# Attention and two feed-forward layers on one core: state products and attention steps moved within a block

## The chip, the core and the metric

One Trainium2 chip, one of its cores. The metric is the device time of one execution in microseconds (us). The kernel's time before is 1480.17 us, the median of three runs (1479.89 to 1481.52).

## The reference

An attention of tokens against 32 state vectors per head, and back, followed by two feed-forward layers over all 8 x 544 = 4352 rows, all in float32:

```python
# x: B=8, H=8, S=512, D=64; state: B, H, Ns=32, D
scores = scale * x @ state.T;    a  = softmax(scores)   # over the 32 states
xread  = a @ state
scores2 = scale * state @ x.T;   a2 = softmax(scores2)  # over the 512 tokens
sread  = a2 @ x
y = concat([xread, sread], axis=2)      # (B, H, 544, 64) -> (4352, 512)
y = (silu(y @ w_gate) * (y @ w_val)) @ w_out            # 512 -> 1536 -> 512
h = y @ w_in
y = (max(h, 0) + alpha * min(h, 0)) @ w_out2            # 512 -> 2048 -> 512
```

## The kernel before

Each large product is made of three passes over float32 values split in two parts (hi and lo, fp32r), so every operand is copied to a hi part by ScalarE (ACT) and its rest is subtracted by VectorE (DVE) or GpSimd (POOL). The first feed-forward layer runs in nine blocks: blocks 0 to 7 are the eight batches with 512 token rows each, the last one holds the 256 rows of sread. The second layer follows and is not touched.

In a block the first layer's input is never formed. Since xread is a @ state, the block multiplies state with the weights first (the **state products**: state_times_w, L381 on TensorE, into two aux buffers of PSUM; then ScalarE's copies and VectorE's subtractions make sw) and then sw with a. Two hidden columns of 128 form a column pair j, and sw of pair j serves steps 2j and 2j+1.

A block has twelve steps f (Block from L397, ffn1 from L445). A step is, on TensorE: gate (6 matmuls into g, L410), value (6 into v, L410), and project (12 matmuls into acc0 to acc3, L434) of the step before. On the other engines: ScalarE's SiLU of g (s, L417), VectorE's product with v (L420), ScalarE's hi part of the hidden column (h, L76), VectorE's lo part (h, L82). Step 0 finishes the block before instead: its last project, then four copies of its accumulators (xo, two by VectorE, L79, two by ScalarE, L76) and their stores. The next block's first project starts new sums in the same four accumulators.

All else is put into slots (f, 0) behind the gate, (f, 1) behind value and split, and (f, 2) behind project. ffn1_slots (from L509) fills them for a block b: state_times_w of pairs 1 to 5 and, at (10, 2), of pair 0 of the next block; the **attention of the next batch** in two head groups u and v, each in five stages: x transposed (xt, L147), scores (L152) with their maxima and exponentials, the scalings with the transposes of the second softmax (L201, aux, then e2t by VectorE), sread (L211), and the split of a (at, a). Blocks 2 to 6 also convert the second layer's weights (raw L246 and L247 on ScalarE, m L252 and L254 on VectorE, L262 on POOL) and split them (sc L329, sp).

TensorE's order is the program's order (manual_schedule). ScalarE, VectorE, POOL and SP get an order from the tile framework's scheduler, which is fixed when the kernel is built; each engine runs its own row in order. aux has two buffers used in turn by state products, scores, transposes and sread; g, v and each accumulator have one.

Of the kernel before, what the change touches and what calls it, by code (L numbers as in the profile page):

```python
# [25 lines left out]
def attention_and_two_ffns(ctx: ExitStack, tc: tile.TileContext, x, state, w_gate, w_val,  # L26
# [76 lines left out]
    def load_state(b, eng=nc.sync):  # L103
        t = sm.tile([P, H, Ns], F32, tag="st", name=name("st"), bufs=1)
        for hp in range(2):
            for e in range(2):
                q = 64 * hp + 32 * e
                eng.dma_start(t[q:q + 32], state[b, :, :, 32 * e:32 * e + 32].rearrange("h n d -> n h d"))
        for hp in range(2):
            q = slice(64 * hp, 64 * hp + 64)  # L110
            for jj in range(2):
                h = 4 * jj + 2 * hp
                nc.vector.transpose(out=bd[b % 2][q, jj, :, Ns * hp:Ns * hp + Ns], in_=t[q, h:h + 2])
        stt[b] = sm.tile([P, H, Ns], F32, tag="stt", name=name("stt"), bufs=2)
        nc.vector.transpose(out=stt[b].rearrange("p h n -> p (h n)"), in_=t.rearrange("p h n -> p (h n)"))

    def load_xq(b, g, jj):
        t = t2([P, S // 32, 32], F32, "xq")
        for hp in range(2):
            for e in range(2):  # L120
                q = 64 * hp + 32 * e
                nc.sync.dma_start(
                    t[q:q + 32],
                    x[b, 4 * jj + 2 * hp + g].rearrange("(t i) d -> i t d", i=32)[:, :, 32 * e:32 * e + 32])
        xq[b, g, jj] = t

    def load_xn(b, g):
        t = t4([P, SC, 4, D], F32, "xn")
        for h in range(4):
            nc.sync.dma_start(t[:, :, h], x[b, 2 * h + g].rearrange("(p c) d -> p c d", c=SC))  # L130
        xn[b, g] = t
# [257 lines left out]
    def state_times_w(b, j):  # L389
        us = [StateTimesW(b, j, g) for g in range(NG)]  # L390
        for u in us:
            u.product()
        for u in us:
            u.parts()
# [70 lines left out]
    with tc.manual_schedule(engines={mybir.EngineType.PE}):  # L465
# [43 lines left out]
        def ffn1_slots(b):  # L509
            slots = {}  # L510

            def put(f, i, th):
                slots.setdefault((f, i), []).append(th)

            if b == 0:
                for f in range(NF1):
                    for i in range(3):
                        put(f, i, stream1.step)
                    if f % 2 == 1:
                        put(f, 1, lambda f=f: stream1.until(3 * (f // 2) + 2, 2))  # L520
                for g in range(NG):
                    put(0, 0, att[0, g].second_scale)
                    put(0, 1, att[0, g].second_read)
            for j in range(1, NJ1):
                if b == 0:
                    put(2 * j - 1, 2, lambda j=j: stream1.until(3 * j + 1, 1))
                    put(2 * j - 1, 2, lambda j=j: state_times_w(0, j))
                else:
                    put(2 * j - 1, 1, lambda j=j: state_times_w(b, j))
            if b == 1:  # L530
                put(8, 0, lambda: stream2.load(1))
            if 1 < b < B - 1:
                for f in range(NF1):
                    if f % 3 != 0:
                        put(f, 1, stream2.step)
                    put(f, 2, one_later)
            if b == B - 1:
                for f in range(NF1):
                    put(f, 2, one_later)
                gen = load_xs()  # L540
                for f in range(4, 8):
                    put(f, 0, lambda: next(gen))
                put(NF1 - 3, 1, lambda: split_w(0))
                put(NF1 - 2, 1, lambda: split_w(1))
            if b + 1 < B:
                nb = b + 1
                put(0, 0, lambda: load_state(nb))
                u, v = att[nb, 0], att[nb, 1]
                for g in range(NG):
                    def load(g=g):  # L550
                        if nb >= XT:
                            for jj in range(2):
                                load_xq(nb, g, jj)
                        load_xn(nb, g)

                    put(*((2 * g, 2 * g) if b == 0 else (6 * g, 0)), load)
                stages = [[lambda: u.xt(0), lambda: u.xt(1)],
                          [u.scores, u.first_cols, u.second_max, u.first_max, u.second_exp, u.first_exp],
                          [u.first_scale, u.second_scale], [u.second_read], [u.first_parts],
                          [lambda: v.xt(0), lambda: v.xt(1)],  # L560
                          [v.scores, v.first_cols, v.second_max, v.first_max, v.second_exp, v.first_exp],
                          [v.first_scale, v.second_scale], [v.second_read], [v.first_parts]]
                if b == 0:
                    places = [(f, 0) for f in range(5)] + [(6, 1), (7, 0), (8, 1), (9, 0), (9, 2)]
                else:
                    places = [(f, 0) for f in (1, 2, 3, 4, 5, 7, 8, 9, 10, 11)]
                for place, stage in zip(places, stages):
                    for th in stage:
                        put(*place, th)
                put(NF1 - 2, 2, lambda: state_times_w(nb, 0))  # L570
            return slots
# [12 lines left out]
        def load_xs():  # L584
            if not xs:
                xs.append(t8([P, NPAIR, 2, NS], F32R, "xs"))
            for r in range(NS // P):
                t = t2([P, DM], F32, "xsn")
                nc.sync.dma_start(t, srd[r * P:(r + 1) * P, :])
                yield  # L590
                pt = aux([P, NPAIR, P])
                for c in range(NPAIR):
                    nc.tensor.transpose(pt[:, c, :], t[:, c * P:(c + 1) * P], ident)
                acopy(xs[0][:, :, 0, r * P:(r + 1) * P], pt)
                sub_lo(xs[0][:, :, 1, r * P:(r + 1) * P], pt, xs[0][:, :, 0, r * P:(r + 1) * P])
                yield

        def split_w(f):
            t = t8([P, NPAIR, 2, 2, P], F32R, "ws")
            src = wraw[f // 2][:, :, :, (f % 2) * P:(f % 2) * P + P]  # L600
            acopy(t[:, :, 0], src)
            sub_lo(t[:, :, 1], src, t[:, :, 0])
            ws[f] = t

        blocks = [block(b) for b in range(B)]
        for b in range(B):
            ffn1(blocks[b], ffn1_slots(b), (lambda: blocks[b - 1].finish(b - 1)) if b else None)
# [203 lines left out]
        for t, (pr, s) in enumerate(STEPS):  # L811
# [5 lines left out]
            todo, places = list(work), [0]  # L817
# [46 lines left out]
```

## Time and profile before

| | us |
|---|---|
| median of three runs | 1480.17 |
| the profiled execution, its own time | 1480.67 |
| its span | 1478.8 |
| TensorE busy (share of the span) | 1420.6 (96%) |
| VectorE busy | 960.4 (65%) |
| ScalarE busy | 525.0 (35%) |
| POOL busy | 209.6 (14%) |

The span is from the first to the last instruction. A timeline row gives start, length, engine, line, output and input, and in brackets the idle time just before it with what ended it. Matmul lengths are modelled and overlap, so the distance between the starts of two rows says more than a length. An engine's share over the whole span mixes stages: the table says which engine to look at, and the timeline where it waits.

### The profile page before, as it was taken

The numbers are of one execution on the slowest core, as the hardware profiler recorded it, in microseconds if no ns is written. First come the engines' busy times: TensorE is split into PE (matmuls) and PEld (weight loads), VectorE is DVE, ScalarE is ACT, GpSimd is POOL, SyncE is SP. The second block draws the span as 40 slices with busy tenths as digits, with TensorE's granted clock in tenths as the row PEclk, the third lists the DMA queues.
The fourth block names the chain that finished last, engine by engine and source line by source line (L and its number), as shares of the span: only waits on it lengthen the run. The fifth ranks groups of instructions, "written<-read, shape, count | busy, mean of one in ns | idle before, by whom it ended". The sixth has DMA issues, their size and how long they took to land.

```text
span 1478.8 us, 18980 instructions
## 1 busy us (share of the span) xinstructions
PE 1420.6 (96%) x7352; PEld 1105.9 (75%) x7352; DVE 960.4 (65%) x1583; ACT 525.0 (35%) x826; POOL 209.6 (14%) x173
## 2 busy tenths in 40 slices
PE   4888999999999999999999999999999999999997
PEld 1556777667677666777997888888888888888886
DVE  6797545676667777533656678666885669666663
ACT  4874445455455544433522112211221113211111
POOL 4686001222233323100000000000000000000000
PEclk6898999999999999999999999999999999999999
DMA  8351223365544544310255433653256434634455
GB/s 273 110 200 34 58 52 105 101 182 172 146 156 150 165 141 139 87 44 1 86 213 217 160 107 116 226 214 132 99 199 232 156 107 164 218 135 152 138 208 210
DMA packets 160595, 214.65 MB, mean 145 GB/s; under 512 B 103160, under 2 KB 104184, under 8 KB 155384
## 3 DMA queue, kind: packets, MB, share of 16 engines
q1 hardware_dynamic: 159416, 213.30, 42.9%
q8 instruction: 58, 0.95, 0.3%
q14 instruction: 33, 0.27, 0.1%
q10 hardware_dynamic: 1088, 0.13, 0.1%
HBM read 169.88 MB, written 43.52 MB: 144 GB/s over the span
## 4 chain that ended last, share of the span: by engine, by line
PE 86%; DVE 9%; issue 1%; ACT 1%; DMA 1%; SPq 0%; DVEq 0%; ACTq 0%
PE acc L434 17%; PE acc L739 13%; PE aux L739 12%; PE g L410 9%; PE v L687 9%; PE v L410 8%; PE aux L687 6%; PE g L687 6%; PE aux L381 3%; DVE m L252 2%; DVE m L254 2%; PE aux L152 1%; DVE sc L329 1%; PE v L789 1%; PE g L789 1%
## 5 line engine op out<-in xcount | busy, mean ns | idle before, releaser
L434 PE MATMUL acc<-h,wp 128*128 128x512 f32 (+1 forms) x1296 | 306.4, 386 | 8.4 <-ACT xo L76 8.4
L434 PEld LDWEIGHTS acc<-h,wp 128*128 128x128 f32 x1296 | 234.9, 191 | 83.0 <-issue 21.0
L76 ACT ACTIVATE h<-m 128x512 fp32r<-128x512 f32 (+1 forms) x144 | 87.6, 609 | 448.3 <-DVE m L672 443.6
L739 PE MATMUL acc<-wo,h 128*128 128x512 f32 x864 | 219.9, 390 | 2.0 <-ACT h L76 1.7
L739 PE MATMUL aux<-wo,h 128*128 128x512 f32 x768 | 194.9, 389 | 0.0
L739 PEld LDWEIGHTS acc<-wo,h 128*128 128x128 f32 x864 | 161.1, 188 | 35.5 <-ACT h L76 2.1
L693 DVE TENSOR_TENSOR u<-v,p 128x512 f32<-128x512 f32 x96 | 66.3, 690 | 168.4 <-PE v L687 167.8
L739 PEld LDWEIGHTS aux<-wo,h 128*128 128x128 f32 x768 | 144.1, 188 | 30.0
L410 PE MATMUL g<-a,sw 128*128 128x512 f32 x576 | 154.5, 403 | 9.2 <-ACT sw L76 6.7
L410 PE MATMUL v<-a,sw 128*128 128x512 f32 x576 | 156.5, 408 | 0.0
L420 DVE TENSOR_TENSOR s<-s,v 128x512 f32<-128x512 f32 (+1 forms) x108 | 70.0, 648 | 121.4 <-PE v L410 111.6
L687 PE MATMUL v<-x,w 128*128 128x512 f32 x576 | 146.2, 389 | 0.0
L410 PEld LDWEIGHTS g<-a,sw 128*128 128x128 f32 x576 | 109.3, 193 | 47.0 <-ACT sw L76 13.0
L410 PEld LDWEIGHTS v<-a,sw 128*128 128x128 f32 x576 | 108.3, 194 | 33.9 <-issue 10.5
L687 PEld LDWEIGHTS v<-x,w 128*128 128x128 f32 x576 | 108.1, 188 | 22.5
L417 ACT ACTIVATE s<-g 128x512 f32<-128x512 f32 (+1 forms) x108 | 62.0, 574 | 146.7 <-PE g L410 140.6
L82 DVE TENSOR_TENSOR h<-m,h 128x512 fp32r<-128x512 f32 (+1 forms) x144 | 94.7, 658 | 16.1 <-ACT h L76 12.8
L76 ACT ACTIVATE h<-s 128x512 fp32r<-128x512 f32 (+1 forms) x108 | 65.4, 606 | 103.1 <-DVE s L420 103.1
L82 DVE TENSOR_TENSOR sw<-aux,sw 128x512 fp32r<-128x512 f32 x96 | 63.2, 681 | 53.2 <-ACT sw L76 53.1
L687 PE MATMUL g<-x,w 128*128 128x512 f32 x384 | 97.6, 389 | 0.0
L687 PE MATMUL aux<-x,w 128*128 128x512 f32 x384 | 97.4, 389 | 0.0
L82 DVE TENSOR_TENSOR h<-s,h 128x512 fp32r<-128x512 f32 (+1 forms) x96 | 66.7, 695 | 35.8 <-ACT h L76 33.3
(105 smaller groups left out, 1656.8 us busy)
## 6 DMA issues: line engine op xcount, KB each, us to landing
w<-w2d SPq DMA_DIRECT2D x64, 896.0 KB, 6.4
wo<-wo2d SPq DMA_DIRECT2D x40, 1024.0 KB, 6.8
w2d<-sp SPq DMA_DIRECT2D x32, 512.0 KB, 2.9
raw<-in_moe_w_out_dram SPq DMA_DIRECT2D x14, 1024.0 KB, 7.8
out_dram<-o SPq DMA_DIRECT2D x34, 256.0 KB, 2.3
xn<-in_x_dram SPq DMA_DIRECT2D x64, 128.0 KB, 3.0
x2d<-xo SPq DMA_DIRECT2D x32, 256.0 KB, 2.5
raw<-in_moe_w_in_dram SPq DMA_DIRECT2D x8, 1024.0 KB, 9.8
```

Source lines behind the costliest of these rows:

```text
L76: return nc.scalar.activation(o, i, AF.Copy)
L82: (eng or nc.vector).tensor_tensor(out=o, in0=src, in1=hi.bitcast(F32), op=ALU.subtract)
L252: nc.vector.tensor_scalar(out=m, in0=hi, scalar1=0x0FFFFFFF, scalar2=3, op0=ALU.bitwise_and, op1=ALU.logical_shift_left)
L254: nc.vector.scalar_tensor_tensor(out=m, in0=hi, scalar=-0x80000000, in1=m, op0=ALU.bitwise_and, op1=ALU.bitwise_or)
L381: nc.tensor.matmul(self.o[Ns * c:Ns * (c + 1), :], stt[b][q, 2 * c + g, :], wraw[j][q, c].rearrange("p k f -> p (k f)"), start=True, stop= ...
L410: nc.tensor.matmul(o[:, :self.n], self.lhs(f, k, a, which), self.rhs(k, c), start=(i == 0), stop=(i == last))
L417: nc.scalar.activation(self.p[f], self.product(f, 0, "g"), AF.Silu)
L420: nc.vector.tensor_tensor(out=self.p[f], in0=self.p[f], in1=self.product(f, 1, "v"), op=ALU.mult)
L434: nc.tensor.matmul(self.acc[e][:, :self.n], wo1[f // 2][:, f % 2, a, e * P:(e + 1) * P], t[:, c, :self.n], start=(f == 0 and i == 0), stop ...
L687: nc.tensor.matmul(o, w[a][:, q, c], x[k][:, q, e], start=start and n == 0, stop=stop and n == 5, skip_group_check=True)
L693: nc.vector.tensor_tensor(out=o, in0=x0, in1=x1, op=ALU.add)
L739: nc.tensor.matmul(o, h[:, c, a, u * P:(u + 1) * P], wos2[t][:, f, q], start=start and f == 0 and i == 0, stop=stop and f == 1 and i == 2)
```

## The change

Two places in ffn1_slots, and nothing else. For blocks 1 to 7 the state products of pair j stand in slot (2j-2, 2), behind the project of the even step before, instead of (2j-1, 1); for j = 1 that is behind the copies of the finished block's sums in the program. For blocks 1 to 6 the attention's ten stages go from steps 1, 2, 3, 4, 5 and 7, 8, 9, 10, 11 to 2, 3, 5, 6, 6 and 6, 7, 9, 10, 10, and the second head group's loads of x go from step 6 to step 4. Block 0 keeps its order.

```diff
                 else:
-                    put(2 * j - 1, 1, lambda j=j: state_times_w(b, j))
+                    put(2 * j - 2, 2, lambda j=j: state_times_w(b, j))
...
-                    put(*((2 * g, 2 * g) if b == 0 else (6 * g, 0)), load)
+                    put(*((2 * g, 2 * g) if b == 0 else (4 * g, 0)), load)
...
                 else:
-                    places = [(f, 0) for f in (1, 2, 3, 4, 5, 7, 8, 9, 10, 11)]
+                    places = [(f, 0) for f in (2, 3, 5, 6, 6, 6, 7, 9, 10, 10)]
```

TensorE in block 4, steps 0 and 1, before, from the gate of step 0 to the first project of the block (acc with the numbers 478 to 481 are the sums of block 3, 617 begins those of block 4):

```order
L410 MATMUL g_3339<-a_519_2909,sw_3273 128x512 x6
L410 MATMUL v_3373<-a_519_2909,sw_3273 128x512 x6
L434 MATMUL acc_478_2683<-h_3309,wp_1111 128x512 x3
L434 MATMUL acc_479_2684<-h_3309,wp_1111 128x512 x3
L434 MATMUL acc_480_2685<-h_3309,wp_1111 128x512 x3
L434 MATMUL acc_481_2686<-h_3309,wp_1111 128x512 x3
L410 MATMUL g_3413<-a_519_2909,sw_3273 128x512 x6
L410 MATMUL v_3425<-a_519_2909,sw_3273 128x512 x6
L381 MATMUL aux_3437<-wr_296,stt_2580 32x512 x4
L381 MATMUL aux_3442<-wr_296,stt_2580 32x512 x4
L434 MATMUL acc_617_3459<-h_3381,wp_298 128x512 x3
```

The same stretch with the change:

```order
L410 MATMUL g_3339<-a_532_2985,sw_3277 128x512 x6
L410 MATMUL v_3373<-a_532_2985,sw_3277 128x512 x6
L434 MATMUL acc_476_2679<-h_3309,wp_1111 128x512 x3
L434 MATMUL acc_477_2680<-h_3309,wp_1111 128x512 x3
L434 MATMUL acc_478_2681<-h_3309,wp_1111 128x512 x3
L434 MATMUL acc_479_2682<-h_3309,wp_1111 128x512 x3
L381 MATMUL aux_3409<-wr_296,stt_2580 32x512 x4
L381 MATMUL aux_3414<-wr_296,stt_2580 32x512 x4
L410 MATMUL g_3428<-a_532_2985,sw_3277 128x512 x6
L410 MATMUL v_3436<-a_532_2985,sw_3277 128x512 x6
L434 MATMUL acc_615_3455<-h_3381,wp_298 128x512 x3
```

The two products L381 moved from behind step 1's gate and value to ahead of them. ScalarE's row of this stretch has the two sw copies, then the two xo copies, then step 1's SiLU, before and with the change.

ScalarE in block 4, from the SiLU of step 2 (g_3480) to the parts sp of step 3, before:

```order
L417 ACTIVATE s_3479<-g_3480 128x512
L194 ACT_TABLE_LOAD
L194 ACTIVATE e_628_3499,r_629_3500<-aux_3488,m_626_3493 128x512
L167 ACTIVATE s_625_3491<-s_625_3491 128x512
L76 ACTIVATE h_3511<-s_3479 128x512
L417 ACT_TABLE_LOAD
L417 ACTIVATE s_3535<-g_3536 128x512
L76 ACTIVATE sw_3569<-aux_3570 128x512
L76 ACTIVATE h_3566<-s_3535 128x512
L76 ACTIVATE sw_3569<-aux_3575 128x512
L76 ACTIVATE sp_3596<-sc_3530 128x512
```

The same stretch with the change, from the SiLU of step 2 (g_3476); e and r belong to the scores of step 3:

```order
L417 ACTIVATE s_3475<-g_3476 128x512
L76 ACTIVATE h_3496<-s_3475 128x512
L417 ACTIVATE s_3535<-g_3536 128x512
L76 ACTIVATE sw_3515<-aux_3516 128x512
L76 ACTIVATE sw_3515<-aux_3521 128x512
L194 ACT_TABLE_LOAD
L194 ACTIVATE e_637_3555,r_638_3556<-aux_3544,m_635_3549 128x512
L167 ACTIVATE s_634_3547<-s_634_3547 128x512
L76 ACTIVATE h_3567<-s_3535 128x512
L76 ACTIVATE sp_3582<-sc_3530 128x512
```

The exponentials moved from step 2 to step 3, and the sw copies of pair 2 stand behind the SiLU of step 3, ahead of the exponentials. Blocks 3 and 5 have this row too; in blocks 1, 2 and 6 the two sw copies stand ahead of step 3's SiLU. VectorE's row with the change has, in blocks 3 to 6, six operations on the second layer's weights (L252, L329, L254, L329, L329, L329) between the hidden part of step 2 and the subtractions of these sw copies.

ScalarE in block 4 with the change, from the SiLU of step 4 (g_3593) to that of step 5 (g_3668):

```order
L417 ACTIVATE s_3592<-g_3593 128x512
L246 ACTIVATE raw_3447<-raw_3447 128x1024
L76 ACTIVATE h_3624<-s_3592 128x512
L247 ACTIVATE raw_3447<-raw_3447 128x1024
L76 ACTIVATE sw_3647<-aux_3648 128x512
L246 ACTIVATE raw_3627<-raw_3627 128x1024
L76 ACTIVATE sw_3647<-aux_3653 128x512
L247 ACTIVATE raw_3627<-raw_3627 128x1024
L417 ACTIVATE s_3667<-g_3668 128x512
```

The same stretch before, from the SiLU of step 4 (g_3607) to that of step 5 (g_3675):

```order
L417 ACTIVATE s_3606<-g_3607 128x512
L246 ACTIVATE raw_3649<-raw_3649 128x1024
L247 ACTIVATE raw_3649<-raw_3649 128x1024
L76 ACTIVATE h_3646<-s_3606 128x512
L417 ACTIVATE s_3674<-g_3675 128x512
```

The first sw copy of pair 3 moved to behind one pair of raw conversions and ahead of step 5's SiLU; its second copy stands between the next two conversions. Before, these copies came behind step 5's SiLU.

## Rows read from the trace of the kernel before

**Rows 1.** The page, part 1: busy us (share of the span) xinstructions.

```profile
PE 1420.6 (96%) x7352; PEld 1105.9 (75%) x7352; DVE 960.4 (65%) x1583; ACT 525.0 (35%) x826; POOL 209.6 (14%) x173
```

**Rows 2.** Timeline of PE: the first gates of blocks 1, 2, 4, 5 and 7.

```profile
146.54 1.52 PE L410 MATMUL g<-a,sw 128*128 128x512 f32 x6
...
224.46 1.52 PE L410 MATMUL g<-a,sw 128*128 128x512 f32 x6
...
387.46 1.52 PE L410 MATMUL g<-a,sw 128*128 128x512 f32 x6
...
472.47 1.52 PE L410 MATMUL g<-a,sw 128*128 128x512 f32 x6
...
641.25 1.52 PE L410 MATMUL g<-a,sw 128*128 128x512 f32 x6
```

**Rows 3.** Timeline of PE: first projects of blocks 3, 4, 6; at 390.18 block 3's last.

```profile
315.20 3.00 PE L434 MATMUL acc<-h,wp 128*128 128x512 f32 x12 [2.11 <-ACT xo L76]
...
390.18 2.88 PE L434 MATMUL acc<-h,wp 128*128 128x512 f32 x12
...
398.91 4.57 PE L434 MATMUL acc<-h,wp 128*128 128x512 f32 x12 [2.11 <-ACT xo L76]
...
568.99 4.34 PE L434 MATMUL acc<-h,wp 128*128 128x512 f32 x12 [2.10 <-ACT xo L76]
```

**Rows 4.** Timeline of ACT, block 4, step 1: copies of sums.

```profile
396.84 1.08 ACT L76 ACTIVATE sw<-aux 128x512 fp32r<-128x512 f32 x2 [4.47 <-PE aux L381]
397.81 1.09 ACT L76 ACTIVATE xo<-acc 128x512 f32<-128x512 f32 x2
```

**Rows 5.** Windows behind the waits: stretch, busy us per engine (x instructions), PEclk, DMA, GB/s.

```profile
315.00:320.00 5.00, 4.80 (x22) 3.51 (x22) 4.67 (x9) 2.24 (x5) 0.00 (x0) 1.00 0.90 313
...
400.00:405.00 5.00, 5.00 (x17) 3.66 (x18) 3.37 (x6) 1.28 (x3) 0.00 (x0) 0.70 1.05 340
```

**Rows 6.** Timeline of PE: products in block 1; scores and products in block 4.

```profile
207.64 1.09 PE L381 MATMUL aux<-wr,stt 64*32 64x512 f32 x16
...
404.77 1.08 PE L152 MATMUL aux<-xt,bd 128*64 128x512 f32 x4
...
445.03 1.85 PE L152 MATMUL aux<-xt,bd 128*64 128x512 f32 x4
...
455.68 1.06 PE L381 MATMUL aux<-wr,stt 64*32 64x512 f32 x8 [0.28 <-DVE e2t L79]
```

**Rows 7.** Timelines of PE, ACT and DVE, block 4, from the products of step 10.

```profile
465.87 1.09 PE L381 MATMUL aux<-wr,stt 64*32 64x512 f32 x16
466.88 1.65 PE L410 MATMUL g<-a,sw 128*128 128x512 f32 x6
...
467.06 1.09 ACT L76 ACTIVATE sw<-aux 128x512 fp32r<-128x512 f32 x2 [2.02 <-PE aux L381]
468.63 0.60 ACT L417 ACTIVATE s<-g 128x512 f32<-128x512 f32 x1 [0.49 <-PE g L410]
...
467.69 1.29 DVE L82 TENSOR_TENSOR sw<-aux,sw 128x512 fp32r<-128x512 f32 x2 [1.93 <-ACT sw L76]
```

**Rows 8.** Timeline of DVE, block 4: first and last of six operations in a row.

```profile
408.98 0.93 DVE L252 TENSOR_SCALAR m<-raw 128x512 int32<-128x512 int32 x1
...
411.03 1.40 DVE L329 TENSOR_TENSOR sc<-m,sc 128x128 f32<-128x128 f32 x1
```

**Rows 9.** Timeline of ACT, block 4, steps 2 and 3, around the exponentials.

```profile
408.54 1.28 ACT L194 ACT_TABLE_LOAD   x1 [3.07 <-DVE m L189]
409.83 0.69 ACT L194 ACTIVATE e<-aux,m 128x512 f32<-128x512 f32 x1
...
412.97 0.60 ACT L417 ACTIVATE s<-g 128x512 f32<-128x512 f32 x1
...
416.30 0.62 ACT L76 ACTIVATE sp<-sc 128x512 fp32r<-128x512 f32 x1
...
417.44 1.15 ACT L246 ACTIVATE raw<-raw 128x1024 f32<-128x1024 f32 x1
```

## The prediction

> **What bounds the kernel now.** The page comes first. TensorE is busy for 96% of the span [rows 1], so a change of order can only win TensorE's waits, its slow clock, and what a late second operand adds inside a group.
>
> The PE timeline gives these block by block. Each of the blocks 1 to 6 issues the same TensorE work, and its length is the distance between the first gates of two blocks. Block 1 takes 224.46 - 146.54 = 77.92 us and has no wait in it. Block 4 takes 472.47 - 387.46 = 85.01 us. The five blocks 2 to 6 together take 641.25 - 224.46 = 416.79 us, and five times 77.92 is 389.60: **27.2 us are lost in them** [rows 2]. That is all this change can win.
>
> Where it goes: in step 1 of block 4 the first projection of the block starts 2.11 us late, released by ScalarE's copies xo, and its 12 matmuls then take 4.57 us where others take 2.88. Block 3 has the same wait without the slow part [rows 3]; block 6 looks like block 4 (2.10 and 4.34 us), and block 5 repeats block 4. ScalarE shows why. It stood idle for 4.47 us until the state products L381 were done, copied their two sums (sw), and only then copied xo [rows 4]. The block's sums were complete when the last projection ended, before step 1's gate; the copies that free them stand behind copies whose data comes two products later. The slow part is the clock: 0.70 of full speed in the 5 us after the wait of block 4, thus mostly the 1.2 GHz level, against 1.00 after that of block 3 [rows 5].
>
> The rest is lost around the attention's steps. The 16 matmuls of L381 run through in 1.09 us in block 1; in step 9 of block 4 their second half waits until VectorE has copied e2t out of the other aux buffer. Block 4's scores take 1.08 us in step 2 and 1.85 in step 8, where their second half waits [rows 6].
>
> **The change, part by part.** No instruction is added or removed. The state products of pair j go from the middle of step 2j-1 to the end of step 2j-2; the attention's steps go to 2, 3, 5, 6, 6, 6, 7, 9, 10, 10; the second head group's loads go from step 6 to step 4.
>
> *The copy wait goes.* With the products directly behind the last projection, gate and value of step 1 lie between them and the next projection. From an existing place with products ahead of a gate: products at 465.87, gate at 466.88, ScalarE's copies at 467.06 (1.19 us after the products), VectorE's subtractions at 467.69 [rows 7]. With 0.5 us between ScalarE's copies, xo is copied 2.1 to 3.2 us after the products start; VectorE's two copies follow its two subtractions (1.8 and 2.4 us after the products), the first ending at some 3.65 us. The projection wants it at 1.0 + 1.5 + 1.4 = 3.9 us. That is covered by 0.2 us; the next three accumulators have 0.7 us more each. Gain: four waits, 8.4 us, and the slow clock behind three of them, 1.69 + 1.69 + 1.46 = 4.8 us, together 13.2.
>
> *The attention's waits go.* No L381 follows transposes within a step any more, and transposes come two steps after their scores. That is the other 27.2 - 13.2 = 14.0 us. Part of it comes back, as follows.
>
> *A new wait at step 3.* Products fill both aux buffers at the end of step 2, and the scores of step 3 want the older one after a single gate. In blocks 3 to 5 ScalarE's row has step 3's SiLU ahead of the sw copies. By rows 7 the SiLU starts 468.63 - 465.87 = 2.76 us after the products, the first copy 0.5 us later, the subtraction that frees the buffer 0.63 us after that and 0.69 us long: free at 4.6 us. TensorE is there at 466.88 + 1.49 - 465.87 = 2.5 us. So the **scores wait 2.1 us in each of three blocks, 6.3 us**. This follows from the order and the rows, so I give it no lower end. In block 6 the copies stand ahead of the SiLU, but VectorE's subtractions stand behind six operations on the second layer's weights, which took 411.03 + 1.40 - 408.98 = 3.45 us in block 4 [rows 8]; without the stretched ones about 1.9 us. That ends 2 to 3.6 us after the products, the buffer is free at 2.6 to 4.3: between 0 and 1.8 us of wait; I take 1.2, nearer to the measured row. In blocks 1 and 2 neither stands in the way: nothing.
>
> *Steps 5, 7 and 9.* The same pair of buffers meets the transposes of 5 and 9 and the scores of 7. At step 5 ScalarE has, from the exponentials of step 3 on, two table loads, two exponentials, a hidden half and a SiLU (412.97 + 0.5 - 408.54 = 4.9 us [rows 9]), three parts of split weights (417.44 - 416.30 = 1.1), another hidden half (0.5) and two raw conversions (1.15 each, about 1.05 from start to start), 8.6 us. It starts 408.54 - 404.77 = 3.8 us after the scores, or 3.2 where no weight operation of VectorE's comes between, so it reaches the copy at 11.8 to 12.4. TensorE issues the products 1.0 + 1.5 + 2.7 + 1.4 + 1.4 + 2.8 = 10.8 us after the scores (scores, value, projection, gate, value, projection), and their sums are there 1.1 us later, at 11.9. So 0 to 0.5 us late; steps 7 and 9 come to 0 to 0.6. Nine places in blocks 3 to 5: 0 to 5.4 us; I take 0.2 each, 1.8.
>
> A rule speaks against this term. Here a table load takes 1.28 us and the exponential behind it starts 0.01 us after its end [rows 9]. The Trainium skill, page "ScalarE: Activation LUTs", section "What ACT_TABLE_LOAD costs", puts a drain of about 1380 ns beside the 1283 ns of every switch. The trace agrees with the load and shows no drain; with it the copies of steps 5 and 9 would come some 2.8 us later. I keep the row.
>
> *The clock.* Of the four waits of 2.1 us, three were followed by the slow level. Of the three new ones I take two, at 1.69 us: 3.4 us; the ends are none, and all four (with block 6), 6.8 us.
>
> *Queues.* The second group's loads are wanted two steps after their issue instead of one, each step being some 7 us (85.01 / 12). SP's queue holds them behind the same stores of split weights as before. That costs nothing; if the stores were late, x's transposes of step 6 and then the scores of step 7 would be. POOL's subtract and scale keep their neighbours and have a step more.
>
> **Sum.** 27.2 - 6.3 - 1.2 - 1.8 - 3.4 = **14.5 us won**. The profiled execution took 1480.67 us (span 1478.8): 1466.2. It lies 0.5 us above the median: **1465.7 us**. Its own ends: 27.2 - 6.3 = 20.9 won, 1459.3; and 27.2 - 6.3 - 1.8 - 5.4 - 6.8 = 6.9 won, 1473.3.
>
> **Rivals.**
> 1. *The scores do not wait.* If the buffer they take were free already, the 1.2 and 1.8 us of the other terms stay at most: 27.2 - 3 = 24 won, **1456**. Against it: the products take both buffers just before.
> 2. *The copy wait stays.* The change promises to free the accumulators in time, yet ScalarE and VectorE still have sw ahead of xo in every block but the last. If those copies come as late as before, the 13.2 us stay lost and 1.3 us are won: **1479**. For it: a cover of only 0.2 us. Against it: the products are 2.8 us earlier, and a miss of that cover costs tenths.
> 3. *ScalarE loses steps 5, 7 and 9: slower.* If there, too, the SiLU or the raw conversions run first, nine places lose 2.1 us and half of them the clock, 2.1 + 0.8 = 2.9 each, 26 us against 14.5 + 1.8: **1490**. It decides from (14.5 + 1.8) / 9 = 1.8 us a place. For it: at step 5 ScalarE arrives within half a microsecond of being late. Against it: its rows have the copies ahead of the SiLU there.
> 4. *A table switch costs twice its load.* Two more loads of 1.28 us ahead of the copies of steps 5 and 9, six places in blocks 3 to 5: 15.4 us, **1481**. Against it: the 0.01 us of rows 9. This is what the Trainium skill's drain ("ScalarE: Activation LUTs") would amount to.
>
> **How the numbers follow.** A measurement of this kernel tells 0.2%, 3 us, from no change. Forecast 0.74; rival 1 0.08, rival 2 0.07, rival 3 0.07, rival 4 0.04. Forecast and rival 1 are faster: 0.82; rivals 2 and 4 make no difference: 0.11; rival 3 is slower: 0.07. The forecast's ends with rival 1 hold 0.82, so the range goes from 1456 to 1474.
>
> **What would show it.** In step 1 of blocks 3 to 6 the first projection has no idle time from xo and takes 2.9 us. In step 3 of blocks 3 to 5 the scores wait some 2.1 us for VectorE's sw, in block 6 less, in blocks 1 and 2 not. No L381 waits for e2t. Blocks 1 and 2 take 77.9 us, blocks 3 to 5 some 81 to 83, block 6 about 79. It is wrong if the scores of step 3 don't wait, if xo still ends a wait of TensorE, or if steps 5, 7 or 9 lose more than a microsecond.

## The result and the profile after

The changed kernel takes **1467.6 us**, the median of four runs (1466.17 to 1469.5), against 1480.03 of the kernel before in the same set of runs (1479.11 to 1481.52): the ratio is 0.9916, with a 95% interval of 0.9899 to 0.9933. That is 12.4 us won; 14.5 were forecast, and the time lies inside the range of 1456 to 1474.

The profiled execution took 1469.5 us, with a span of 1467.3. The page, part 1, of the changed kernel, to be set beside [rows 1]:

```profile
PE 1408.8 (96%) x7352; PEld 1100.2 (75%) x7352; DVE 963.7 (66%) x1583; ACT 524.3 (36%) x826; POOL 210.8 (14%) x173
```

TensorE has the same 7352 matmuls and is busy 11.8 us less, though its share of the span is the same 96%: what the slow clock and late operands added inside groups counted as busy time, too. Windows from the first gate of block 2 to that of block 7, before and after (stretch, busy us of PE, PEld, DVE, ACT and POOL, PEclk, DMA, GB/s):

```profile
224.46:641.25 416.79, 406.06 (x2321) 288.76 (x2320) 278.42 (x506) 209.88 (x344) 108.43 (x94) 0.99 0.44 136
...
225.72:629.77 404.05, 393.59 (x2321) 283.00 (x2320) 279.52 (x506) 208.34 (x344) 109.70 (x94) 1.00 0.46 141
```

TensorE's idle time in these five blocks is 416.79 - 406.06 = 10.7 us before and 404.05 - 393.59 = 10.5 after. The change took the old waits away and made new ones of nearly the same sum; what was won is busy time that the slow clock and stretched groups (as the scores of step 8, 1.85 us where others take 1.08 [rows 6]) had cost. The share hides this; the distances between blocks show the gain. The timeline of PE with the first gates of blocks 1, 2, 4, 5 and 7, as in [rows 2]:

```profile
147.60 1.52 PE L410 MATMUL g<-a,sw 128*128 128x512 f32 x6
...
225.72 1.52 PE L410 MATMUL g<-a,sw 128*128 128x512 f32 x6
...
385.56 1.52 PE L410 MATMUL g<-a,sw 128*128 128x512 f32 x6
...
468.87 1.52 PE L410 MATMUL g<-a,sw 128*128 128x512 f32 x6
...
629.77 1.52 PE L410 MATMUL g<-a,sw 128*128 128x512 f32 x6
```

Blocks 2 to 6 take 629.77 - 225.72 = 404.05 us, where they took 416.79: 12.7 won. Block 4 takes 83.31, where it took 85.01. Blocks 1 and 2, which have no wait now, take 78.12 and 78.10, so the new order costs 0.2 us a block by itself. Block 1 starts 1.06 us later than before; block 0 was not changed, and in a second profile of the same kernel (experiment 8) block 1 starts at 146.93, so this is the spread of the beginning.

What is left of the loss, 404.05 - 5 x 77.92 = 14.4 us, is four kinds of waits. The timeline of PE, steps 3, 7 and 9 of block 3, then step 3 of blocks 4 to 6:

```profile
326.12 1.08 PE L152 MATMUL aux<-xt,bd 128*64 128x512 f32 x4 [1.90 <-DVE sw L82]
...
354.10 1.08 PE L152 MATMUL aux<-xt,bd 128*64 128x512 f32 x4 [0.82 <-DVE sw L82]
...
367.94 0.72 PE L201 MATMUL aux<-ident,e 128*128 128x128 f32 x4 [0.41 <-DVE sw L82]
...
407.84 1.93 PE L152 MATMUL aux<-xt,bd 128*64 128x512 f32 x4 [1.90 <-DVE sw L82]
409.70 2.40 PE L410 MATMUL v<-a,sw 128*128 128x512 f32 x6
...
491.14 1.08 PE L152 MATMUL aux<-xt,bd 128*64 128x512 f32 x4 [1.90 <-DVE sw L82]
...
571.97 1.08 PE L152 MATMUL aux<-xt,bd 128*64 128x512 f32 x4 [0.97 <-DVE sw L82]
```

The scores of step 3 wait 1.90 us in blocks 3 to 5 and 0.97 in block 6, always for VectorE's sw. In block 4 alone the scores themselves then take 1.93 us where others take 1.08, and value 2.40: the slow clock. Steps 7 and 9 of blocks 4 and 5 look like those of block 3 (0.83 and 0.90 us, 0.41 and 0.42). No first project of a block waits, and no L381 waits for e2t.

### The profile page after: what moved, and what is told of

Its sections match the earlier page's. It is cut to its first block, busy times and chain, and to the rows that moved or that the text cites. A ratio compares the mean times of both kernels' runs of the same rounds, so it can differ in the third digit from the quotient of the medians.

```text
span 1467.3 us, 19014 instructions
## 1 busy us (share of the span) xinstructions
PE 1408.8 (96%) x7352; PEld 1100.2 (75%) x7352; DVE 963.7 (66%) x1583; ACT 524.3 (36%) x826; POOL 210.8 (14%) x173
## 4 chain that ended last, share of the span: by engine, by line
PE 83%; DVE 10%; ACT 4%; issue 2%; DMA 1%; SPq 0%; DVEq 0%; ACTq 0%
PE acc L434 14%; PE acc L739 13%; PE aux L739 12%; PE v L687 9%; PE v L410 9%; PE g L410 8%; PE aux L687 6%; PE g L687 6%; PE aux L381 2%; DVE m L252 2%; DVE m L254 2%; PE aux L152 1%; DVE sw L82 1%; PE v L789 1%; PE g L789 1%
## 5 line engine op out<-in xcount | busy, mean ns | idle before, releaser
L434 PE MATMUL acc<-h,wp 128*128 128x512 f32 (+1 forms) x1296 | 298.2, 379 | 0.0
L410 PE MATMUL g<-a,sw 128*128 128x512 f32 x576 | 158.1, 408 | 9.7 <-ACT sw L76 6.4
L410 PEld LDWEIGHTS g<-a,sw 128*128 128x128 f32 x576 | 105.6, 191 | 74.2 <-issue 28.5
L82 DVE TENSOR_TENSOR h<-s,h 128x512 fp32r<-128x512 f32 (+1 forms) x96 | 63.3, 659 | 40.6 <-ACT h L76 38.3
```

Source lines behind the costliest of these rows:

```text
L82: (eng or nc.vector).tensor_tensor(out=o, in0=src, in1=hi.bitcast(F32), op=ALU.subtract)
L410: nc.tensor.matmul(o[:, :self.n], self.lhs(f, k, a, which), self.rhs(k, c), start=(i == 0), stop=(i == last))
L434: nc.tensor.matmul(self.acc[e][:, :self.n], wo1[f // 2][:, f % 2, a, e * P:(e + 1) * P], t[:, c, :self.n], start=(f == 0 and i == 0), stop ...
```

## The experiments

The theory to be tested has three parts. ScalarE, VectorE and TensorE each run their own row in order, so a wait is set by what stands ahead of the sw copies in a row, and not only by when the products come. The move of the products frees the accumulators. The attention's new places are what keeps the aux buffers from meeting once the products have moved. The earlier loads of x belong to the second edit and were not tested apart from it. The rivals: that one of the two edits is the whole gain; that the products still come too late for the scores; that ScalarE's own backlog from the exponentials makes the late waits. Where nothing else is said, an experiment differs from the changed kernel by the lines shown. Experiments 1 to 4, 5 to 8 and 9 were run in three further sets, in which the kernel before took 1479.9, 1480.97 and 1481.12 us, where it took 1480.03 beside the changed kernel: a difference between runs of two sets can be off by about 1 us.

**1. The products alone** (difference to the kernel before):

```diff
-                    put(2 * j - 1, 1, lambda j=j: state_times_w(b, j))
+                    put(2 * j - 2, 2, lambda j=j: state_times_w(b, j))
```

> The state products at the end of even steps, the attention's steps and the loads as before the change. Theory: the two edits buy different things, and this one frees the accumulators. The first project of blocks 3 to 6 waits 0 for xo (13.2 us of waits and slow clock won). The transposes of steps 3 and 9 now stand right behind the products, whose copies stand behind two exponentials in ScalarE's row (and behind a raw conversion at step 9): they wait some 0.5 to 1.3 us at step 3 and 1.5 to 2.4 at step 9 for VectorE's sw, 10 to 20 us with the clock. Total 1463 to 1473. Rival (the products' move is all of the gain, the attention's move is idle): no new waits at steps 3 and 9, about 1455 to 1460. Rival (the attention's move is the gain): 1475 or more, with the wait for xo still there.

Measured: 1473.15 us, ratio 0.995 (0.9935 to 0.9965). The wait for xo is gone: step 1 of blocks 3 to 6 takes 5.61 to 5.63 us, with no idle time. The transposes of steps 3 and 9 wait instead; the timeline of PE, block 5, steps 3 and 9:

```profile
494.11 0.75 PE L201 MATMUL aux<-ident,e 128*128 128x128 f32 x4 [1.20 <-DVE sw L82]
...
535.63 0.72 PE L201 MATMUL aux<-ident,e 128*128 128x128 f32 x4 [1.71 <-DVE sw L82]
```

Both are at the places and of about the size worked out from ScalarE's row. The products' move alone is worth 6.8 us, about half of the pair's 12.4, so it is not the whole gain.

**2. The attention alone** (difference to the kernel before):

```diff
-                    put(*((2 * g, 2 * g) if b == 0 else (6 * g, 0)), load)
+                    put(*((2 * g, 2 * g) if b == 0 else (4 * g, 0)), load)
...
-                    places = [(f, 0) for f in (1, 2, 3, 4, 5, 7, 8, 9, 10, 11)]
+                    places = [(f, 0) for f in (2, 3, 5, 6, 6, 6, 7, 9, 10, 10)]
```

> The attention's steps and the loads moved, the state products as before the change. Theory: the wait for xo stays (2.1 us in blocks 3 to 6, slow clock behind most). Scores and products now share steps 3 and 7, and the second half of the products wants the scores' buffer, which the exponential frees some 4.5 us after the scores, while TensorE is there after 3.0: 1.5 us at two steps of five blocks, 15 us, in place of the 14.0 lost at steps 2, 3, 8, 9 before. Total 1478 to 1492, no gain or slower. Rival (moving the attention apart wins its share by itself): 1466 to 1469.

Measured: **1535.62 us**, ratio 1.0392 (1.0361 to 1.0422): 55.7 us slower, far more than expected. The place was right; the timeline of PE, block 4, step 3:

```profile
437.84 1.06 PE L381 MATMUL aux<-wr,stt 64*32 64x512 f32 x8
441.81 1.93 PE L381 MATMUL aux<-wr,stt 64*32 64x512 f32 x8 [2.91 <-ACT e L194]
443.68 4.73 PE L434 MATMUL acc<-h,wp 128*128 128x512 f32 x12
```

The second half of the products waits for the exponential that reads the scores, as expected, but 2.91 us and not 1.5, because VectorE's weight operations stand ahead of the maxima. Then the clock falls: the granted clock is 0.54 in the 7 us from 441 to 448, near the 1.2 GHz level, and the next project takes 4.73 us. Step 5 loses more, since the SiLU and the hidden part stand behind the second sw copy there: TensorE waits 1.44 us in the products and 1.72 and 1.67 in the project, and the step takes 15.12 us. So the attention's new places are not a gain of their own: they are good only behind moved products.

**3. The SiLU of step 3 behind the copies.** ScalarE's row changes in blocks 3 to 5 by this one instruction; the rows of the other engines stay as they are.

```diff
-            acopy(t[:, self.g, 0], self.o)
+            copied[self.b, self.j] = acopy(t[:, self.g, 0], self.o)
...
+    behind = lambda b, f: tc.issue_after(copied[b, 2].ins) if f == 3 and 1 < b < B - 1 else nullcontext()
...
-            nc.scalar.activation(self.p[f], self.product(f, 0, "g"), AF.Silu)
+            with behind(self.b, f): nc.scalar.activation(self.p[f], self.product(f, 0, "g"), AF.Silu)
```

> The changed kernel with one difference: in step 3 of blocks 2 to 6 ScalarE's SiLU has to come behind the two sw copies of pair 2; the rows of the other engines are the same. Theory (the wait at step 3 is made by that SiLU): the scores' wait in blocks 3 to 5 falls from 1.90 us to 0.9 to 1.0, where VectorE's six weight operations end it as in block 6 (0.97 there, unchanged). 2.8 us won, with the slow clock of block 4 up to 4.5: 1463 to 1465. Rival (the products simply come too late for the scores): 1.9 us stays, 1467.6. Rival (the SiLU made late delays the step): the value's product and the next project wait, no gain or slower.

Measured: 1463.29 us, ratio 0.9881 (0.9867 to 0.9894), 4.3 us under the changed kernel. The changed kernel's timelines of ACT and DVE, block 4, step 3:

```profile
405.97 0.60 ACT L417 ACTIVATE s<-g 128x512 f32<-128x512 f32 x1 [3.90 <-PE g L410]
406.46 1.08 ACT L76 ACTIVATE sw<-aux 128x512 fp32r<-128x512 f32 x2
...
404.85 1.39 DVE L329 TENSOR_TENSOR sc<-m,sc 128x128 f32<-128x128 f32 x1
407.09 1.29 DVE L82 TENSOR_TENSOR sw<-aux,sw 128x512 fp32r<-128x512 f32 x2 [0.85 <-ACT sw L76]
```

And those of PE, ACT and DVE of experiment 3 at the same place:

```profile
404.47 1.08 PE L152 MATMUL aux<-xt,bd 128*64 128x512 f32 x4 [0.97 <-DVE sw L82]
...
401.95 1.09 ACT L76 ACTIVATE sw<-aux 128x512 fp32r<-128x512 f32 x2 [2.32 <-PE aux L381]
403.53 0.60 ACT L417 ACTIVATE s<-g 128x512 f32<-128x512 f32 x1 [0.49 <-PE g L410]
...
402.41 1.40 DVE L329 TENSOR_TENSOR sc<-m,sc 128x128 f32<-128x128 f32 x1
403.74 1.28 DVE L82 TENSOR_TENSOR sw<-aux,sw 128x512 fp32r<-128x512 f32 x2
```

In the changed kernel ScalarE idles 3.90 us for the gate, the last 1.6 of them with the products' sums ready (their matmuls end at 403.26 + 1.09 = 404.35), and VectorE then idles 0.85 us for the copy. With the copies ahead, the subtraction starts as soon as the last of the six weight operations ends. The wait is 0.97 us in all four blocks, and no block shows the slow clock: 3 x 0.93 of waits and the 1.6 of block 4's clock are the 4.3 us. What makes the difference between 1.90 and 0.97 is the SiLU; this is shown.

**4. The products earlier, ahead of the project:**

```diff
-                    put(2 * j - 2, 2, lambda j=j: state_times_w(b, j))
+                    put(2 * j - 2, 1, lambda j=j: state_times_w(b, j))
```

> The changed kernel with the products of even steps ahead of the project instead of behind it, 2.8 us earlier. Theory (the order of ScalarE's row decides, not when the products come): the SiLU of step 3 is still ahead of the copies in blocks 3 to 5, so the scores of step 3 still wait 1.9 us there; the copies ahead of step 7 still stand behind the hidden part of step 6, so 0.8 us stays there; the wait at step 9 (0.41) and that of block 6 at step 3 (0.97) go. Some 2.6 us won: 1465. Rival (the products come too late): 2.8 us more cover everywhere, all waits go, 13 us won: 1455.

Measured: 1476.41 us, ratio 0.9973 (0.9964 to 0.9982): 8.8 us *slower* than the changed kernel, where a gain of 2.6 us was expected. The timeline of PE, block 4, steps 2, 3 and 7, and that of ACT at step 3:

```profile
400.94 1.09 PE L381 MATMUL aux<-wr,stt 64*32 64x512 f32 x16
...
408.25 1.08 PE L152 MATMUL aux<-xt,bd 128*64 128x512 f32 x4 [1.90 <-DVE sw L82]
...
439.30 1.16 PE L152 MATMUL aux<-xt,bd 128*64 128x512 f32 x4 [2.52 <-DVE sw L82]
...
406.39 0.60 ACT L417 ACTIVATE s<-g 128x512 f32<-128x512 f32 x1 [3.92 <-PE g L410]
406.88 1.08 ACT L76 ACTIVATE sw<-aux 128x512 fp32r<-128x512 f32 x2
```

The products start 408.25 - 400.94 = 7.3 us before the scores, where it was 4.6 in the changed kernel, and the wait is the same 1.90 us to the hundredth: the copies start when the SiLU is done, whenever the sums came. The waits at step 9 and in block 6 went, as expected. The wait at step 7 did not stay at 0.83 but grew to 2.52, and the slow clock follows it in all three blocks. There the split of a now stands between the hidden part of step 6 and the sw copies in ScalarE's row (in the changed kernel it ran ahead of the hidden part, in idle time), and both of VectorE's subtractions stand behind a part of split weights that takes 1.67 us. With earlier products the scheduler made a worse row.

**5. Step 6 made lighter:**

```diff
-                    places = [(f, 0) for f in (2, 3, 5, 6, 6, 6, 7, 9, 10, 10)]
+                    places = [(2, 0), (3, 0), (5, 0), (6, 0), (8, 0), (5, 2), (7, 0), (9, 0), (10, 0), (10, 0)]
```

> The changed kernel with two stages moved out of step 6: the transposes of the second head group's x go to the end of step 5, the split of the first group's a to step 8. Theory (the wait of the scores at step 7 comes from VectorE's row: the product s of step 6 stands behind a stretched subtraction and three transposes of step 6, ScalarE's hidden part behind that product, the sw copies behind the hidden part): the wait at step 7 in blocks 3 to 5, 0.83 us now, goes to 0 to 0.2; step 3 keeps its 1.90 and step 9 its 0.4. Steps 6 and 7 together 1.0 us shorter in three blocks: about 3 us won, 1464.5. Rival (ScalarE's own backlog from the exponentials makes it): 0.8 stays, 1467.6.

Measured: 1471.47 us, ratio 0.993 (0.9914 to 0.9946). The changed kernel's timelines of DVE and ACT, block 4, steps 6 and 7, show what was tested:

```profile
430.97 1.79 DVE L82 TENSOR_TENSOR sp<-sc,sp 128x512 fp32r<-128x512 f32 x1
432.68 0.70 DVE L179 STREAM_TRANSPOSE at<-s 128x512 f32<-128x512 f32 x1
433.39 0.71 DVE L147 STREAM_TRANSPOSE xt<-xq 128x512 f32<-128x512 f32 x1
434.03 0.65 DVE L420 TENSOR_TENSOR s<-s,v 128x512 f32<-128x512 f32 x1
...
434.76 0.63 ACT L76 ACTIVATE h<-s 128x512 fp32r<-128x512 f32 x1 [0.71 <-DVE s L420]
435.29 0.62 ACT L76 ACTIVATE sp<-m 128x512 fp32r<-128x512 f32 x1
435.81 1.06 ACT L76 ACTIVATE sw<-aux 128x512 fp32r<-128x512 f32 x2
```

The product s of step 6 stands behind a subtraction and two transposes on VectorE; ScalarE's hidden part waits for it, and the sw copies stand behind the hidden part. With two stages out of step 6 the wait at step 7 is gone in blocks 3 to 5, so this chain is shown and ScalarE's backlog from the exponentials is not its cause. But the gain was given back: the split of a, now in step 8, comes ahead of the next sw copies in ScalarE's row, VectorE takes their subtractions behind more operations on the weights, step 9 waits 1.38 us and not 0.41, and in block 6 the gate of step 7 waits 1.18 us for the SiLU of step 6, which stands behind a sw copy. The median is 3.9 us above the changed kernel's, and 2.6 above its one run in the same set (experiment 8); of the two profiles, blocks 1 to 6 differ by 1.6 us (483.74 to 482.17), and the run that was profiled is the shortest of the five, 1467.95. Where the rest lies is open.

**6. Experiment 3, with the weight step out of step 2** (difference to experiment 3):

```diff
-                    if f % 3 != 0:
+                    if f in (1, 3, 4, 5, 7, 8, 10, 11):
```

> The kernel of the third experiment (SiLU behind the copies) with the second layer's weight step of step 2 moved to step 3. Theory (VectorE's six weight operations make what is left of the wait at step 3): the 0.97 us of blocks 3 to 6 goes to 0 to 0.2 in all four, 3 to 4 us won against the third experiment's 1463.3: about 1459.5. The moved operations and parts now stand ahead of the sw copies of step 4 in ScalarE's row: up to 1 us may come back at step 5 in three blocks. Rival (the products come too late for the scores): 0.97 stays.

Measured: 1460.17 us, ratio 0.9863 (0.9847 to 0.9878). The 0.97 us at step 3 is gone in all four blocks (6.82 us in place of 7.84), and so are the waits of steps 7 and 9. At step 5 of blocks 4 and 5 a new one stands, 1.73 and 1.72 us, for VectorE's hidden part: ScalarE's row of these two blocks now has the hidden part of step 4 behind three raw conversions, the sw copies and the SiLU of step 5, which waits for its gate. Step 4 of blocks 3 to 6 takes some 0.5 us more. The scores of step 3 in block 4 on PE, with no idle time ahead:

```profile
400.82 1.08 PE L152 MATMUL aux<-xt,bd 128*64 128x512 f32 x4
```

Both parts of the theory of step 3 hold: the SiLU makes half of that wait, VectorE's weight operations the other half. The total is as expected in part by luck: the gains at steps 6, 7 and 9 (4.8 us by the steps' lengths) and the losses at steps 4 and 5 (5.8) nearly cancel. Those gains come from rows that the scheduler changed along the way: at step 6 of block 3 VectorE's subtraction of 1.79 us is no longer ahead of the product s, which starts 4.6 us after that step's gate and not 6.6. That fits experiment 5; what freed step 9 was not tested.

**7. All together.** Experiment 6 with the lines of 4 and 5. ScalarE's row then has the sw copies ahead of the SiLU at steps 3, 5, 7 and 9.

> All together: products of even steps ahead of the project, SiLU of step 3 behind the copies, weight step out of step 2, second group's transposes and first group's split out of step 6. ScalarE's row then has the sw copies ahead of the SiLU at steps 3, 5, 7 and 9. Theory: with the rows in that order and 2.8 us more of cover no wait is left at steps 3, 5, 7, 9; each of the blocks 2 to 6 takes some 78.0 us (77.96 in blocks 2 and 6 of the fourth experiment), 9.6 us less than in the third: 1453.7. Rival (a queue not yet seen becomes the bound): waits of over 0.5 us at one of these steps, 1457 or more.

Measured: **1454.38 us** (1452.8 to 1456.11), ratio 0.982 (0.9804 to 0.9836), the best of all: 26.6 us under the kernel before and 13.2 under the changed one. Step 3 of block 4 on PE:

```profile
400.06 1.52 PE L410 MATMUL g<-a,sw 128*128 128x512 f32 x6
401.51 1.08 PE L152 MATMUL aux<-xt,bd 128*64 128x512 f32 x4
```

No matmul of blocks 1 to 6 has idle time of 0.15 us or more ahead of it, and the blocks take 77.96, 78.24, 77.99, 77.96, 77.96 and 77.96 us. Blocks 2 to 6 take 390.1 us together, where five times 77.92 is 389.6: of the 27.2 us that [rows 2] show as lost this order wins all but 0.5.

**8. The changed kernel once more**, nothing altered:

> The changed kernel unaltered, for a second profile. The waits are set by the rows and come back the same: 1.90 at step 3 of blocks 3 to 5, 0.97 in block 6, 0.8 at step 7, 0.4 at step 9. If the slow clock behind a wait of 1.9 us is a matter of chance it need not be in block 4 alone this time: total 1466 to 1470.

Measured, one run: 1468.87 us. The waits came back at the same places: 1.90 three times, 0.97, 0.83 to 0.89, 0.42 to 0.45. The slow clock came back as well, but in block 3 and not in block 4. Windows behind the wait of block 3 and of block 4 in this profile:

```profile
325.00:330.00 5.00, 4.55 (x12) 2.46 (x13) 3.20 (x7) 0.63 (x2) 0.60 (x1) 0.66 0.25 74
...
408.00:413.00 5.00, 4.25 (x18) 2.90 (x19) 3.82 (x7) 1.46 (x2) 1.05 (x1) 1.00 0.61 211
```

In the first profile it was the other way round:

```profile
407.00:412.00 5.00, 4.16 (x11) 2.14 (x12) 3.23 (x6) 0.62 (x3) 0.20 (x1) 0.66 0.58 199
...
326.00:331.00 5.00, 4.88 (x21) 3.42 (x22) 3.19 (x7) 1.62 (x2) 1.05 (x1) 1.00 0.29 92
```

**9. Experiment 7 with the products behind the project again**, thus experiment 6 with the line of 5 alone:

> The seventh experiment without one of its parts: the products of even steps stand behind the project again, as in the change. Theory (each sw copy has to stand ahead in ScalarE's row and its products early enough for that; one without the other is not enough): here the copies of step 8 stand behind the split of a, two raw conversions, a hidden part and a part of split weights, so step 9 waits 1.4 to 2.0 us in blocks 3 to 5, and step 5's late hidden part of the sixth experiment (1.7 us in two blocks) stays; no waits at steps 3 and 7. Some 10 us more than the seventh's 1454.4: 1461 to 1466. Rival (the repaired rows of steps 3 and 7 are all of the gain, the 2.8 us are idle): 1454 to 1456.

Measured: 1466.61 us, ratio 0.9905 (0.9891 to 0.992), 12.2 us above experiment 7. Step 9 waits 1.54 to 1.57 us in blocks 3 to 5, step 5 of blocks 4 and 5 waits 1.75 and 1.73 for the hidden part, and steps 3 and 7 wait for nothing, as expected; the total is 0.6 us above the expected range. Step 9 of block 4 on PE:

```profile
448.43 0.72 PE L201 MATMUL aux<-ident,e 128*128 128x128 f32 x4 [1.54 <-DVE sw L82]
```

The same 2.7 us of earlier products that lost 8.8 us in experiment 4 win 12.2 here: what they are worth is decided by the rows. Experiment 6, without the line of 5, had no wait at step 9 and took 6.4 us less than this one. Experiment 6 with the line of 4 alone was not run, so whether experiment 7 needs the line of 5 is open.

## Why the prediction was right, point by point

- *The copy wait goes: right.* Step 1 of block 4 in the changed kernel, on PE, ACT and DVE:

```profile
391.10 1.09 PE L381 MATMUL aux<-wr,stt 64*32 64x512 f32 x16
394.99 2.91 PE L434 MATMUL acc<-h,wp 128*128 128x512 f32 x12
...
393.19 1.10 ACT L76 ACTIVATE xo<-acc 128x512 f32<-128x512 f32 x2
...
394.06 1.28 DVE L79 COPY xo<-acc 128x512 f32<-128x512 f32 x2
```

  The first of VectorE's copies ends at some 394.7, 3.6 us after the products start, and the project wants it 3.9 us after: the thin cover of 0.2 to 0.3 us was real, and it held in every block. Experiment 1 shows that this edit alone brings it. Step 1 of blocks 3 to 6 took 8.85, 10.41, 10.37 and 10.14 us before, against 6.70 of block 1, 13.0 us in sum: the 13.2 of the forecast.

- *The attention's waits go, 14.0 us: right in sum, with a condition that the text did not have.* No L381 waits for e2t any more, and what is left of the 27.2 us is accounted for by the points below. Experiment 2 shows that the attention's places do this only together with the moved products.

- *A new wait at step 3: right.* 2.1 us in each of three blocks was forecast from the row and measured as 1.90. The scores of block 4 start 407.84 - 403.26 = 4.58 us after the products, as the 4.6 that was worked out; TensorE was there at 2.7 and not at 2.5. The wait in block 6 was taken at 1.2 and measured as 0.97. Experiments 3, 4 and 6 show the two causes that the text gave, one at a time.

- *Steps 5, 7 and 9: the term that was mis-sized.* 1.8 us was forecast; the waits are 0 at step 5, 2.6 us at the three steps 7 and 1.2 at the three steps 9, and with what they lengthen around them steps 6, 7 and 9 take 4.8 us more. The step that failed is "steps 7 and 9 come to 0 to 0.6": step 7 waited 0.82 to 0.90. The sum stays inside the 0 to 5.4 that the text gave, and no single step 5, 7 or 9 lost the microsecond that would have made it wrong, but step 7 of block 5 came to within 0.02 of it (7.80 us against 6.82 of block 1). Only step 5 had been worked out from its row, and its sum held. Step 7 has other work ahead: VectorE's row of step 6, which got three of the attention's stages at once (experiment 5). Step 9 is rival 3's mechanism in small; ScalarE there in block 4:

```profile
447.69 1.17 ACT L246 ACTIVATE raw<-raw 128x1024 f32<-128x1024 f32 x1
448.74 1.16 ACT L247 ACTIVATE raw<-raw 128x1024 int32<-128x1024 uint32 x1
449.78 1.08 ACT L76 ACTIVATE sw<-aux 128x512 fp32r<-128x512 f32 x2
```

  Two raw conversions run while the products finish, and the copies come behind them. Experiment 4, whose row has the copies of that step ahead of them, shows no wait at step 9.

- *The clock: 3.4 us forecast, 1.6 measured.* One of the three waits was followed by the slow level, not two; block 4's step 3 takes 10.40 us and block 3's 8.78. Which one is not decided by the program alone (experiment 8).

- *Rivals.* Rival 1 (no wait at step 3) and rival 2 (xo still waits) are out by the rows above. Rival 3 (slower by steps 5, 7 and 9) is out as a whole: 4.8 us were lost there, not 26. Rival 4, a switch of tables that costs more than its load, is out too; ScalarE in the changed kernel, block 4:

```profile
411.93 1.28 ACT L194 ACT_TABLE_LOAD   x1 [4.38 <-DVE m L189]
413.23 0.69 ACT L194 ACTIVATE e<-aux,m 128x512 f32<-128x512 f32 x1
...
416.20 1.28 ACT L417 ACT_TABLE_LOAD   x1
417.49 0.60 ACT L417 ACTIVATE s<-g 128x512 f32<-128x512 f32 x1
```

  The exponential starts 0.02 us after the end of its load. ScalarE was idle ahead of that load, but not ahead of the second one, which starts 0.02 us after the end of the copy before it (415.47 + 0.71); its SiLU starts 0.01 us after its end. The drain of about 1380 ns that the Trainium skill, page "ScalarE: Activation LUTs", section "What ACT_TABLE_LOAD costs", puts beside each load does not show here, and the copies of step 5 behind it were in time.

The sum of what stayed lost in blocks 2 to 6, forecast and measured: step 3 6.3 and 5.9, block 6 1.2 and 1.0, steps 5 to 9 1.8 and 4.8, the clock 3.4 and 1.6, and 0.9 us that the forecast did not have, the new order's 0.2 a block. 12.7 became 14.2, by the steps' lengths, beside the 14.4 of the blocks' starts. That the total came so near is in part luck: the 3.0 us too little at steps 5 to 9 and the 0.9 left out were partly made up by a slow clock that cost 1.8 us less than forecast, and waits at step 3 that were 0.6 us shorter. Behind which waits the slow clock comes was a guess.

## What to carry to other kernels

When an instruction is moved to free a buffer sooner, read what stands ahead of the instruction that frees it in *its own engine's row*: the products came 2.7 us earlier in experiment 4 and the wait did not change by a hundredth, while moving one SiLU by two places halved it. Work the same sum out for every place at which the pattern repeats, since the neighbours differ from place to place. Do not count idle time alone: here TensorE was idle in blocks 2 to 6 nearly as long after as before, and the gain was in its busy time. And test two edits of one change alone and together: here they are worth +6.8, -55.7 and, as a pair, +12.4 us.

## What was not expected of the hardware

The same wait of 1.90 us at the same place of the same program is followed by TensorE's slow level (0.66 granted) in one profile and by full speed in another. In the four profiles with that wait (the changed kernel twice, experiments 4 and 5) it was followed by it in 5 of 12 places; after the 2.52 us of experiment 4 in 3 of 3. Each time it cost some 1.6 us more. What decides it stays open; a wait that is taken away takes its share of this with it, as experiment 3 did.
